# Seven block products for the product with w_in, and a cosine from 1 - 2 sin² without a clamp

## The chip, the cores and the metric

The kernel runs on one core of a Trainium2 chip. The metric is device microseconds of one execution, median of the runs shown; lower is better. The profile is taken of one further execution.

## What is computed

Three layers in a row, in fp32, over 4608 tokens of width 512:

```python
# 1. attention in chunks of 64 tokens, 64 (batch, head) pairs, head width 64
attn = softmax(q_c @ k_c.T / 8);  x = attn @ v_c          # -> [4608, 512]
# 2. RMS norm, then a gated layer, d_ff = 1536
xn = x / rms(x) * rms_g
x2 = (silu(xn @ w_gate) * (xn @ w_val)) @ w_out           # -> [4608, 512]
# 3. a cosine gate, d_ff = 2048
h = x2 @ w_in                                             # -> [4608, 2048]
out = (h * cos(h)) @ w_out2                               # -> [4608, 512]
```

The weights arrive in 64 bits and are turned into 32 on the core.

## The kernel before

The work goes in four stages, each of which writes its result to DRAM and the next reads it back: (1) attention, norm and the two gated products (lines L359 to L514); (2) the product with the first w_out (L269 under the pool `ps_c`); (3) the product with w_in and the cosine gate (L656 to L782, L798); (4) the product with the second w_out (pool `ps_c4`, L834 to L881).

Every product is made of three TensorE passes (`mm3`, L269): each fp32 operand is split into a rounded part and a remainder (`split`, L120 and L121, or L256 and L257 in `operand`: ScalarE rounds, VectorE subtracts), and high·high, high·low and low·high are added up in PSUM.

Stages 2 and 4 cut their matrices into 2 x 2 blocks and make seven block products in place of eight (the order is `PRODUCTS`); sums and differences of blocks are made on VectorE (L230 to L253) before the split, and sums of products after it (L713, L721, L841). Stage 2 takes tiles of 768 tokens, so its matmuls have 384 columns; stage 4 has 256 columns.

Stage 3 does not cut. It takes nine tiles of 512 tokens (`TILE`); for each pair of the 16 blocks of 128 rows of w_in it runs 24 matmuls of 512 columns into a PSUM tile of two banks, four such tiles in turn (`ps_h`). w_in was scaled by 1/(2 pi) beforehand (L187), so that h stands in turns. Per pair, `cosine` runs a chain over 128 x 1024 elements:

```python
nc.scalar.activation(k, h, AF.Copy, bias=0.25)                                # L798: nearest whole turn
nc.vector.scalar_tensor_tensor(r, k, -1.0, u, op0=ALU.mult, op1=ALU.add)      # L778: what is left of it
nc.vector.tensor_scalar(r, r, R_MIN, R_MAX, op0=ALU.max, op1=ALU.min)         # L779: the clamp
nc.scalar.activation(r, r, AF.Sin, scale=PI2, bias=halfpi)                    # L780: cos = sin(x + pi/2)
nc.vector.scalar_tensor_tensor(r, u, PI2, r, op0=ALU.mult, op1=ALU.mult)      # L781: h * cos(h)
```

The weights of all later stages are converted during stage 1: `w_tick` takes one raw piece at a time, eight per tile of 512 tokens, and stores the split weight in DRAM (`kept`). For w_in a piece is scaled and split (L187, L120, L121); for the two w_out the block sums are made too (L201). SBUF has 28 places for weights (`p0` to `p27`); the list `wanted` says which tile takes a place as `free` gives it back.

Stage 1 has its order on TensorE and VectorE written out by hand. In stages 2 to 4 a planner orders each engine's instructions when the program is built: it lays them out by durations of its own and gives a free engine the first one in program order that is ready by then. On the chip each engine then runs its list in that order. All DMAs go through SP's queue.

Of the kernel before, what the change touches and what calls it, by code (L numbers as in the profile page):

```python
# [9 lines left out]
F32 = mybir.dt.float32  # L10
# [10 lines left out]
P = 128  # L21
NT = 4608
# [42 lines left out]

BANK = {1: "b1", 6: "b1", 5: "b1", 3: "b1", 2: "b2", 7: "b3", 4: "b4"}
# [5 lines left out]
def kernel(  # L72
# [24 lines left out]
    gd = [dr.tile([P, N2 // 4, 4, TILE], F32, name=f"gd{t}") for t in range(NT // TILE)]  # L97
# [30 lines left out]
    wanted += [("in", f, None) for f in range(4)] + [("x2", 0, c) for c in range(2)]  # L128
    wanted += [("in", f, None) for f in range(4, N2)]
    last = [("out2", g, PLACE_B[j]) for g in range(N2 // 4) for j in PRODUCTS]  # L130
    wanted += last[:10] + [("g", g, c) for g in range(2) for c in range(2)] + last[10:]
    place_of, weight, kept, early = {}, {}, {}, {}

    def free(*tags):
        for tag in tags:
            if not wanted:
                return
            key = kind, i, k = wanted.pop(0)
            place_of[key] = tag
            if kind in ("h", "x2", "g"):  # L140
                early[key] = wp.tile([P, 2, H if kind == "h" else D], F32, tag=tag, name="a")
                rows = slice(0, 2) if kind == "h" else slice(2 * k, 2 * k + 2)
                a = {"h": hd[0][:, k], "x2": x2d[0], "g": gd[0][:, i]}[kind]
                nc.sync.dma_start(out=early[key], in_=a[:, rows, : early[key].shape[-1]])
                continue
            shape = [P, 2, D] if kind == "in" else [P, 2, 2, 2, P]
            weight[key] = wp.tile(shape, F32R, tag=tag, name="w")
            nc.sync.dma_start(out=f32(weight[key]), in_=kept[kind, i] if kind == "in" else kept[kind, i][:, k])
# [4 lines left out]
    todo_w += [("in", f, 0) for f in range(N2)]  # L153
# [4 lines left out]
    def w_load():  # L158
        if todo_w and len(raws) < 2:
# [3 lines left out]
            if kind == "in":  # L163
                nc.sync.dma_start(out=raw, in_=w2[i, 0].rearrange("p (a b) -> p a b", b=P))
# [9 lines left out]
    def w_tick():  # L174
# [9 lines left out]
        if kind == "in":  # L184
            to = pp.tile([P, 2, D], F32R, tag="pout", name="wout")
            t = t.rearrange("p a b -> p (a b)")
            nc.scalar.activation(t, t, AF.Copy, scale=INV2PI)  # L187
            split(to, t, nc.vector)
            kept[kind, i] = dr.tile([P, 2, D], F32, name=f"kin{i}")
            nc.sync.dma_start(out=kept[kind, i], in_=f32(to))  # L190
        else:
            s = pp.tile([P, 4, P], F32, tag="ps", name="wsum")

# [739 lines left out]
```

## Time and profile before

| what | value |
|---|---|
| median of 3 runs | 1741.5 us (1739.72 to 1741.79) |
| the profiled execution | 1740.49 us, span 1738.7 us |
| TensorE busy | 1702.5 us of the span (98%) |
| VectorE, ScalarE, GpSimd busy | 1176.3, 750.7, 60.7 us |
| mean granted TensorE clock | 0.995 of full speed |
| stage 3 on TensorE | from 980.3 to 1372.0 us after the span's start |

Busy time of TensorE counts overlapping matmuls once. The time outside the span, 1.8 us, is what lies before the first and after the last instruction.

### The profile page before, as it was taken

The numbers are of one execution on the slowest core, as the hardware profiler recorded it, in microseconds if no ns is written. First come the engines' busy times: TensorE is split into PE (matmuls) and PEld (weight loads), VectorE is DVE, ScalarE is ACT, GpSimd is POOL, SyncE is SP. The second block draws the span as 40 slices with busy tenths as digits, with TensorE's granted clock in tenths as the row PEclk, the third lists the DMA queues.
The fourth block names the chain that finished last, engine by engine and source line by source line (L and its number), as shares of the span: only waits on it lengthen the run. The fifth ranks groups of instructions, "written<-read, shape, count | busy, mean of one in ns | idle before, by whom it ended". The sixth has DMA issues, their size and how long they took to land.

```text
span 1738.7 us, 29349 instructions
## 1 busy us (share of the span) xinstructions
PE 1702.5 (98%) x11832; PEld 1530.8 (88%) x11832; DVE 1176.3 (68%) x1759; ACT 750.7 (43%) x1115; POOL 60.7 (3%) x104
## 2 busy tenths in 40 slices
PE   4899999999999999999999999999999999999999
PEld 4899888888888888899999988888888999999999
DVE  5775487666687741577777566666676687777775
ACT  4542444445444431344444344444454444444443
POOL 2222000000000000000000000000000000000000
PEclk8999999999999999999999999999999999999999
DMA  9423277656577738553336843333225833444430
GB/s 332 171 68 99 91 241 245 225 175 217 206 236 243 235 104 277 178 182 146 146 146 239 284 155 121 121 121 121 98 90 182 318 113 126 133 147 145 143 128 31
DMA packets 160743, 294.72 MB, mean 170 GB/s; under 512 B 10592, under 2 KB 97632, under 8 KB 156256
## 3 DMA queue, kind: packets, MB, share of 16 engines
q1 hardware_dynamic: 160608, 292.86, 49.3%
q8 instruction: 93, 1.52, 0.4%
q14 instruction: 42, 0.34, 0.1%
HBM read 173.80 MB, written 119.01 MB: 168 GB/s over the span
## 4 chain that ended last, share of the span: by engine, by line
PE 95%; issue 1%; POOL 1%; ACT 1%; DMA 1%; DVE 1%; SPq 0%; POOLq 0%
PE b L269 35%; PE h L269 23%; PE v L269 17%; PE g L269 16%; PE sc L359 1%; PE o L412 1%; PE pt L398 1%; PE tr L450 1%; POOL w L121 1%; DMA qk<-in_qk_dram 1%; DMA w<-kin 0%; POOL rs L430 0%; ACT p L381 0%; ACT L381 0%; ACT xo L256 0%
## 5 line engine op out<-in xcount | busy, mean ns | idle before, releaser
L269 PE MATMUL h<-xt,w 128*128 128x512 f32 x1728 | 391.9, 389 | 0.0
L269 PEld LDWEIGHTS h<-xt,w 128*128 128x128 f32 x1728 | 324.3, 188 | 67.3
L269 PEld LDWEIGHTS b<-w,xo 128*128 128x128 f32 x3024 | 363.0, 192 | 0.1
L269 PE MATMUL b<-w,xo 128*128 128x256 f32 x3024 | 363.0, 283 | 0.0
L269 PE MATMUL v<-xt,w 128*128 128x512 f32 (+1 forms) x1488 | 324.4, 367 | 3.6 <-DVE xn L437 1.8
L269 PE MATMUL g<-xt,w 128*128 128x512 f32 (+1 forms) x1488 | 320.8, 365 | 0.8 <-ACT xt L452 0.7
L269 PEld LDWEIGHTS g<-xt,w 128*128 128x128 f32 x1488 | 257.6, 191 | 44.8 <-ACT xt L452 1.1
L269 PEld LDWEIGHTS v<-xt,w 128*128 128x128 f32 x1488 | 253.7, 191 | 46.1 <-DVE xn L437 2.0
L269 PE MATMUL b<-xo,w 128*128 128x384 f32 x1512 | 263.2, 334 | 3.6 <-ACT xo L256 3.5
L269 PEld LDWEIGHTS b<-xo,w 128*128 128x128 f32 x1512 | 262.1, 188 | 4.7 <-ACT xo L256 4.5
L257 DVE TENSOR_TENSOR xo<-rawg,xo 128x512 fp32r<-128x512 f32 x204 | 135.5, 688 | 66.6 <-ACT xo L256 66.5
L256 ACT CAST xo<-rawg 128x512 fp32r<-128x512 f32 x204 | 121.8, 620 | 126.0 <-PE b L269 82.1
L501 DVE TENSOR_TENSOR h<-sg,v 128x512 f32<-128x512 f32 (+1 forms) x124 | 76.2, 615 | 138.6 <-PE v L269 123.2
L500 ACT ACTIVATE sg<-g 128x512 f32<-128x512 f32 (+1 forms) x124 | 66.9, 541 | 237.1 <-PE g L269 223.5
L780 ACT ACTIVATE r<-r,halfpi 128x1024 f32<-128x1024 f32 x72 | 83.0, 1153 | 134.4 <-DVE r L779 134.2
L781 DVE SCALAR_TENSOR_TENSOR r<-h,r 128x1024 f32<-128x1024 f32 x72 | 88.1, 1224 | 74.2 <-ACT r L780 73.7
L778 DVE SCALAR_TENSOR_TENSOR r<-k,h 128x1024 f32<-128x1024 int32 x72 | 87.9, 1220 | 69.3 <-ACT k L798 69.1
L256 ACT CAST xo<-rawh 128x768 fp32r<-128x768 f32 x102 | 81.3, 834 | 97.4 <-DMA rawh<-hd 53.5
L257 DVE TENSOR_TENSOR xo<-rawh,xo 128x768 fp32r<-128x768 f32 x102 | 92.9, 953 | 40.4 <-ACT xo L256 40.3
L798 ACT ACTIVATE k<-h 128x1024 int32<-128x1024 f32 x72 | 73.9, 1026 | 79.5 <-PE h L269 79.5
L256 ACT CAST xo<-tmp 128x512 fp32r<-128x512 f32 (+1 forms) x54 | 37.4, 692 | 61.6 <-DVE tmp L230 36.9
L779 DVE TENSOR_SCALAR r<-r 128x1024 f32<-128x1024 f32 x72 | 49.9, 693 | 2.1
(86 smaller groups left out, 1230.4 us busy)
## 6 DMA issues: line engine op xcount, KB each, us to landing
gd<-r SPq DMA_DIRECT2D x72, 512.0 KB, 2.6
rawg<-gd SPq DMA_DIRECT2D x34, 1024.0 KB, 7.1
kout<-wout SPq DMA_DIRECT2D x56, 448.0 KB, 4.5
w<-kout SPq DMA_DIRECT2D x49, 512.0 KB, 4.9
hd<-h SPq DMA_DIRECT2D x46, 512.0 KB, 4.7
rawh<-hd SPq DMA_DIRECT2D x15, 1536.0 KB, 9.1
qk<-in_qk_dram SPq DMA_DIRECT2D x36, 512.0 KB, 6.1
wraw<-in_w_dram SPq DMA_DIRECT2D x112, 128.0 KB, 2.7
```

Source lines behind the costliest of these rows:

```text
L121: eng.tensor_tensor(to[:, 1], a, f32(to[:, 0]), op=ALU.subtract)
L256: nc.scalar.copy(hi, a)
L257: nc.vector.tensor_tensor(lo, a, f32(hi), op=ALU.subtract)
L269: nc.tensor.matmul(acc, a, b, start=first and k == 0 and q == 0, stop=k == n - 1 and q == 2, skip_group_check=True)
L359: nc.tensor.matmul(sc[part(h ^ b), 2 * hp + (c ^ b), :], t[part(h), 0, hp, part(c)], t[part(h), 1, hp, part(c)], start=True, stop=True,)
L500: nc.scalar.activation(sg, acc[0], AF.Silu)
L501: nc.vector.tensor_tensor(h, sg, acc[1], op=ALU.mult)
L778: nc.vector.scalar_tensor_tensor(r, k, -1.0, u, op0=ALU.mult, op1=ALU.add)
L779: nc.vector.tensor_scalar(r, r, R_MIN, R_MAX, op0=ALU.max, op1=ALU.min)
L780: nc.scalar.activation(r, r, AF.Sin, scale=PI2, bias=halfpi)
L781: nc.vector.scalar_tensor_tensor(r, u, PI2, r, op0=ALU.mult, op1=ALU.mult)
L798: nc.scalar.activation(k, h, AF.Copy, bias=0.25)
```

## The change

Stage 3 is cut like the others. It takes six tiles of 768 tokens, and w_in in four groups of 512 columns of h; for each of the 24 pairs of tile and group (a *group* below) it makes seven block products of 12 matmuls, 384 columns each. The order is 1, then the products 4 and 3 of the group before, then 2, 6, 5, 7. Product sums run up in PSUM bank pair `b1` (1, 1+6, 1+6+7, 1+6+7+4; two buffers), `b2` (2) and `b5` (5, then 5+3; one buffer each). ScalarE copies `b1` out on the way (`z1`, `z16`, `z167`); VectorE adds these to `b2` and `b5` and so gives three of the group's four result blocks, in SBUF; the fourth is `b1` itself. The operands of the next tile's products are made one by one behind the products of the last group of a tile.

For three of the four blocks the cosine is made another way: k is the nearest whole number, q = u - k, then Sin at half the angle, Square, and one VectorE instruction for (2 pi)(2 sin² - 1) u; there is no clamp and no bias. w_in is scaled by -1/(2 pi), so u is minus the turn. The fourth block keeps the old chain. All of these work on 128 x 768 elements.

Preparing w_in now makes the block sums as for the w_out; its weights in SBUF are 28 pieces of 512 KB in place of 16. `gd` is kept in pieces of 1536 tokens in place of 512. The first five operands of stage 4 (`op4`) get places among the weights.

The diff, cut to its core:

```diff
+THIRD = (1, 2, 6, 5, 7, 4, 3)
+BANK3 = {1: "b1", 6: "b1", 7: "b1", 4: "b1", 2: "b2", 5: "b5", 3: "b5"}
...
     x2d = [dr.tile([P, ND, PIECE], F32, name=f"x2d{q}") for q in range(NPIECE)]
-    gd = [dr.tile([P, N2 // 4, 4, TILE], F32, name=f"gd{t}") for t in range(NT // TILE)]
+    gd = [dr.tile([P, N2 // 4, 4, PIECE], F32, name=f"gd{q}") for q in range(NPIECE)]
...
     wanted[3:3] = [("h", 0, g) for g in range(N1 // 4)]
-    wanted += [("in", f, None) for f in range(4)] + [("x2", 0, c) for c in range(2)]
-    wanted += [("in", f, None) for f in range(4, N2)]
+    third_w = [("in", g, PLACE_A[j]) for g in range(N2 // 4) for j in THIRD]
+    wanted += third_w[:7] + [("x2", r, c) for r in range(2) for c in range(2)] + third_w[7:]
     last = [("out2", g, PLACE_B[j]) for g in range(N2 // 4) for j in PRODUCTS]
-    wanted += last[:10] + [("g", g, c) for g in range(2) for c in range(2)] + last[10:]
+    wanted += last[:10] + [("g", g, c) for g in range(2) for c in range(2)]
+    wanted += [("op4", n, None) for n in range(AHEAD)] + last[10:]
...
     todo_w = [("out1", i, half) for i in range(N1 // 2) for half in range(2)]
-    todo_w += [("in", f, 0) for f in range(N2)]
+    todo_w += [("in", i, half) for i in range(N2 // 2) for half in range(2)]
...
             raw = wp.tile([P, 4, P], U64, tag=f"p{24 + flip[0]}", name="wraw")
             if kind == "in":
-                nc.sync.dma_start(out=raw, in_=w2[i, 0].rearrange("p (a b) -> p a b", b=P))
+                m, e = 4 * (i // 2) + half, i % 2
+                for n, (f, c) in enumerate(((m, e), (m, e + 2), (m + 2, e + 2), (m + 2, e))):
+                    nc.sync.dma_start(out=raw[:, n, :], in_=w2[f, 0][:, c * P : (c + 1) * P])
...
         t = f32(t)
         if kind == "in":
-            to = pp.tile([P, 2, D], F32R, tag="pout", name="wout")
-            t = t.rearrange("p a b -> p (a b)")
-            nc.scalar.activation(t, t, AF.Copy, scale=INV2PI)
-            split(to, t, nc.vector)
-            kept[kind, i] = dr.tile([P, 2, D], F32, name=f"kin{i}")
-            nc.sync.dma_start(out=kept[kind, i], in_=f32(to))
+            nc.scalar.activation(t, t, AF.Copy, scale=-INV2PI)
+        s = pp.tile([P, 4, P], F32, tag="ps", name="wsum")
...
+            ops = ((t[:, 3, :], t[:, 0, :], ALU.subtract), (t[:, 2, :], s[:, 0, :], ALU.subtract))
+            ops += ((t[:, 2, :], t[:, 3, :], ALU.subtract), (t[:, 1, :], s[:, 1, :], ALU.subtract))
         else:
...
-                nc.sync.dma_start(out=kept[kind, g][:, :, e, h, half], in_=f32(to[:, h]))
+            ops = ((t[:, 3, :], t[:, 2, :], ALU.add), (s[:, 0, :], t[:, 0, :], ALU.subtract))
+            ops += ((t[:, 0, :], t[:, 3, :], ALU.subtract), (t[:, 1, :], s[:, 1, :], ALU.subtract))
+        for n, (a, b, op) in enumerate(ops):
...
+        to = pp.tile([P, 2, 7, P], F32R, tag="pout", name="wout")
+        split(to[:, :, 0:3, :], t[:, :3, :], nc.vector)
+        split(to[:, :, 3:7, :], s, nc.vector)
...
+    def fetch3(s):
+        if s == 0:
+            raw3[s] = {(r, c): early["x2", r, c] for r in range(2) for c in range(2)}
+        elif s < NB:
+            t = third_p.tile([P, 4, T], F32, tag="raw", name="rawx2", bufs=1)
+            raw3[s] = blocks(t, False)
+            c = s * T % PIECE
+            nc.sync.dma_start(out=t, in_=x2d[s * T // PIECE][:, :, c : c + T])
...
+    def operand3(s, j):
+        b = raw3[s]
+        if j == 6:
+            raw3[s, "t"] = t = third_p.tile([P, 2, H], F32, tag="tmp", name="tmp", bufs=1)
+            nc.vector.tensor_tensor(t, b[0, 1], b[0, 0], op=ALU.subtract)
+            nc.vector.tensor_tensor(b[0, 0], b[1, 1], t, op=ALU.subtract)
+        elif j == 7:
+            nc.vector.tensor_tensor(b[0, 1], b[1, 1], b[0, 1], op=ALU.subtract)
+        elif j == 4:
+            nc.vector.tensor_tensor(b[1, 0], b[1, 0], b[0, 0], op=ALU.subtract)
+        a = raw3[s, "t"] if j == 5 else b[{1: (0, 0), 2: (1, 0), 6: (0, 0), 7: (0, 1), 4: (1, 0), 3: (1, 1)}[j]]
+        pool = third_p if j in (1, 2, 6) else left_p
+        o = pool.tile([P, 2, 2, H], F32R, tag="x3", name="x3", bufs=4)
+        split(o, a, nc.vector)
+        ops3[s, j] = o
+        if j == 3:
+            if s == 0:
+                free(*(place_of["x2", r, c] for r in range(2) for c in range(2)))
+            else:
+                fetch3(s + 1)
+    def ahead3(n):
+        while made3[0] < min(len(seq3), n):
+            operand3(*seq3[made3[0]])
+            made3[0] += 1
...
                     second.close()
-                    xt_p = third.enter_context(tc.tile_pool(name="xt3", bufs=2, side="right", reuse_waits="tile"))
+                    third_p = third.enter_context(tc.tile_pool(name="right3", bufs=1, side="right", reuse_waits="tile"))
                     fetch3(0)
-                    split3(0, 0)
-                    split3(0, 2)
+                    fetch3(1)
+                    ahead3(3)
...
-            nc.sync.dma_start(out=t, in_=gd[s][:, g])
+            c = s * TILE % PIECE
+            nc.sync.dma_start(out=t, in_=gd[s * TILE // PIECE][:, g, :, c : c + TILE])
...
     def operand4(s, j, g):
-        tmp = xo_p.tile([P, 2, H4], F32, tag="tmp", name="tmp", bufs=1) if j == 7 else None
-        ops4[s, j, g] = operand(j, raw4[s, g], tmp, lambda: parts(xo_p, H4), True)
+        n = made4[0]
+        if n < AHEAD:
+            tmp = left_p.tile([P, 2, H], F32, tag="r", name="tmp", bufs=4)[:, :, :H4] if j == 7 else None
+            o = wp.tile([P, 2, 2, H4], F32R, tag=place_of["op4", n, None], name="xo")
+            to = o[:, 0], o[:, 1]
+        else:
+            tmp = xo_p.tile([P, 2, H4], F32, tag="tmp", name="tmp", bufs=1) if j == 7 else None
+            to = parts(xo_p, H4)
+        ops4[s, j, g] = operand(j, raw4[s, g], tmp, lambda: to, True)
...
         st.enter_context(third)
-        tp = st.enter_context(tc.tile_pool(name="tp3", bufs=2, side="right", reuse_waits="tile"))
-        ps_h = st.enter_context(tc.tile_pool(name="ps_h", bufs=4, space=PSUM, reuse_waits="tile"))
...
-        def cosine(keep):
-            while len(late) > keep:
-                u, k, i, f = late.pop(0)
-                r = tp.tile([P, 2, D], F32, tag="r", name="r", bufs=4)
-                nc.vector.scalar_tensor_tensor(r, k, -1.0, u, op0=ALU.mult, op1=ALU.add)
-                nc.vector.tensor_scalar(r, r, R_MIN, R_MAX, op0=ALU.max, op1=ALU.min)
-                nc.scalar.activation(r, r, AF.Sin, scale=PI2, bias=halfpi)
-                nc.vector.scalar_tensor_tensor(r, u, PI2, r, op0=ALU.mult, op1=ALU.mult)
-                nc.sync.dma_start(out=gd[i][:, f // 4, f % 4 : f % 4 + 2, :], in_=r)
...
-        for i in range(ntile):
...
-            for f in range(0, N2, 2):
-                h = ps_h.tile([P, 2, D], F32, tag="h", name="h2")
-                for e in range(2):
-                    w = weight["in", f + e, None]
-                    c = [slice(d * P, (d + 1) * P) for d in range(ND)]
-                    x = xts[i]
-                    mm3(h[:, e], [(w[:, 0, c[d]], w[:, 1, c[d]], x[:, 0, d], x[:, 1, d]) for d in range(ND)], True)
-                k = tp.tile([P, 2, D], I32, tag="k", name="k")
-                nc.scalar.activation(k, h, AF.Copy, bias=0.25)
-                late.append((h, k, i, f))
-                cosine(0)
-                if i == ntile - 1:
-                    free(place_of["in", f, None], place_of["in", f + 1, None])
-                    if f == 0:
+        left_p = st.enter_context(tc.tile_pool(name="left3", bufs=1, reuse_waits="tile"))
+        ps_h = st.enter_context(tc.tile_pool(name="ps_h", bufs=1, space=PSUM, reuse_waits="tile"))
+        ahead3(7)
...
+        def multiply(acc, s, j, g, first):
+            w = weight["in", g, PLACE_A[j]]
+            x = ops3[s, j]
+            for p in range(2):
+                mm3(
+                    acc[:, p],
+                    [(w[:, e, 0, p], w[:, e, 1, p], x[:, 0, e], x[:, 1, e]) for e in range(2)],
+                    first,
+                )
+            if s == NB - 1:
+                free(place_of["in", g, PLACE_A[j]])
+            if g == G3 - 1 and j != 1:
+                ahead3(made3[0] + 1)
...
+        def opened(bank, bufs=1):
+            return ps_h.tile([P, 2, D], F32, tag=bank, name=bank, bufs=bufs)[:, :, :H]
+        def saved(acc, tag):
+            t = left_p.tile([P, 2, H], F32, tag=tag, name=tag)
+            nc.scalar.copy(t, acc)
+            return t
+        def total(acc, part):
+            t = left_p.tile([P, 2, H], F32, tag="u", name="u", bufs=3)
+            nc.vector.tensor_tensor(t, acc, part, op=ALU.add)
+            return t
...
+        def turn(u, s, g, r, c, whole):
+            q = left_p.tile([P, 2, H], F32, tag="r", name="r", bufs=4)
+            k = q.bitcast(I32)
+            if whole:
+                nc.scalar.copy(k, u)
+                nc.vector.scalar_tensor_tensor(q, k, -1.0, u, op0=ALU.mult, op1=ALU.add)
+                nc.scalar.activation(q, q, AF.Sin, scale=math.pi)
+                nc.scalar.activation(q, q, AF.Square, scale=math.sqrt(2 * PI2))
+                nc.vector.scalar_tensor_tensor(q, q, -PI2, u, op0=ALU.add, op1=ALU.mult)
+            else:
+                nc.scalar.activation(k, u, AF.Copy, bias=0.25)
+                nc.vector.scalar_tensor_tensor(q, k, -1.0, u, op0=ALU.mult, op1=ALU.add)
+                nc.vector.tensor_scalar(q, q, R_MIN, R_MAX, op0=ALU.max, op1=ALU.min)
+                nc.scalar.activation(q, q, AF.Sin, scale=PI2, bias=halfpi)
+                nc.vector.scalar_tensor_tensor(q, u, -PI2, q, op0=ALU.mult, op1=ALU.mult)
+            t0 = s * T + c * H
+            o = t0 % PIECE
+            nc.sync.dma_start(out=gd[t0 // PIECE][:, g, 2 * r : 2 * r + 2, o : o + H], in_=q)
...
+        def tail(s, g, z, z16):
+            multiply(z["b1"], s, 4, g, False)
+            turn(z["b1"], s, g, 1, 0, False)
+            multiply(z["b5"], s, 3, g, False)
+            turn(total(z["b5"], z16), s, g, 0, 1, True)
...
+        rest = None
+        for s in range(NB):
+            for g in range(G3):
+                z = {"b1": opened("b1", 2)}
+                multiply(z["b1"], s, 1, g, True)
+                z1 = saved(z["b1"], "z1")
+                if rest:
+                    tail(*rest)
+                z["b2"] = opened("b2")
+                multiply(z["b2"], s, 2, g, True)
+                turn(total(z["b2"], z1), s, g, 0, 0, True)
+                multiply(z["b1"], s, 6, g, False)
+                z16 = saved(z["b1"], "z16")
+                z["b5"] = opened("b5")
+                multiply(z["b5"], s, 5, g, True)
+                multiply(z["b1"], s, 7, g, False)
+                turn(total(z["b5"], saved(z["b1"], "z167")), s, g, 1, 1, True)
+                rest = s, g, z, z16
+                if g == G3 - 2:
+                    ahead3(made3[0] + 1)
+                if s == NB - 1:
+                    if g == G3 - 2:
                         fetch4(0, 0)
                         fetch4(0, 1)
-                    elif f >= 6:
-                        ahead4((f - 4) // 2)
-                if f in (8, 10):
-                    split3(i + 1, f - 8 if f == 8 else 2)
-                if f == 10:
-                    fetch3(i + 2)
-            if i == 0:
-                free(place_of["x2", 0, 0], place_of["x2", 0, 1])
+                        ahead4(2)
+                    elif g == G3 - 1:
+                        ahead4(4)
+        tail(*rest)
+        ahead4(AHEAD)
...
-        st.enter_context(fourth)
...
+        xo_p = st.enter_context(tc.tile_pool(name="xo4", bufs=8, reuse_waits="tile"))
...
+            if n < AHEAD:
+                free(place_of["op4", n, None])
```

## Rows read from the trace of the kernel before

**Rows 1.** The page's first part: busy us, share of the span, instructions, by engine.

```profile
PE 1702.5 (98%) x11832; PEld 1530.8 (88%) x11832; DVE 1176.3 (68%) x1759; ACT 750.7 (43%) x1115; POOL 60.7 (3%) x104
```

**Rows 2.** The chain that ended last, its piece for stage 3: start, us, what.

```profile
980.31 391.72 PE h L269 x1728
```

**Rows 3.** Windows, stages 2 to 4: us, then busy of PE, PEld, DVE, ACT, POOL.

```profile
713.50:980.00 266.50, 262.86 (x1513) 261.89 (x1512) 198.57 (x220) 118.12 (x149) 0.00 (x0) 1.00 0.50 177
980.00:1372.00 392.00, 392.00 (x1732) 324.60 (x1731) 248.39 (x244) 174.66 (x167) 0.00 (x0) 1.00 0.40 145
1372.00:1738.70 366.70, 362.90 (x3025) 362.70 (x3023) 272.68 (x424) 163.67 (x279) 0.00 (x0) 1.00 0.38 132
```

**Rows 4.** Groups by line and form, matmuls and weight loads: busy us, mean ns | idle.

```profile
L269 PE MATMUL h<-xt,w 128*128 128x512 f32 x1728 | 391.9, 389 | 0.0
...
L269 PE MATMUL b<-xo,w 128*128 128x384 f32 x1512 | 263.2, 334 | 3.6 <-ACT xo L256 3.5
L269 PEld LDWEIGHTS b<-xo,w 128*128 128x128 f32 x1512 | 262.1, 188 | 4.7 <-ACT xo L256 4.5
```

**Rows 5.** Groups by line and form: the cosine chain of stage 3, 1024 elements.

```profile
L781 DVE SCALAR_TENSOR_TENSOR r<-h,r 128x1024 f32<-128x1024 f32 x72 | 88.1, 1224 | 74.2 <-ACT r L780 73.7
L778 DVE SCALAR_TENSOR_TENSOR r<-k,h 128x1024 f32<-128x1024 int32 x72 | 87.9, 1220 | 69.3 <-ACT k L798 69.1
L780 ACT ACTIVATE r<-r,halfpi 128x1024 f32<-128x1024 f32 x72 | 83.0, 1153 | 134.4 <-DVE r L779 134.2
...
L798 ACT ACTIVATE k<-h 128x1024 int32<-128x1024 f32 x72 | 73.9, 1026 | 79.5 <-PE h L269 79.5
...
L779 DVE TENSOR_SCALAR r<-r 128x1024 f32<-128x1024 f32 x72 | 49.9, 693 | 2.1
```

**Rows 6.** Groups by line and form: copies and sums of 768, casts of 512 and 1024.

```profile
L256 ACT CAST xo<-rawh 128x768 fp32r<-128x768 f32 x102 | 81.3, 834 | 97.4 <-DMA rawh<-hd 53.5 <-PE b L269 19.7 <-DVE rawh L253 12.5
...
L121 DVE TENSOR_TENSOR xt<-rawx,xt 128x1024 fp32r<-128x1024 f32 x16 | 19.4, 1219 | 1.6 <-ACT xt L120 1.6
...
L721 DVE TENSOR_TENSOR x<-b,s 128x768 f32<-128x768 f32 x18 | 17.2, 955 | 9.9 <-ACT s L711 5.2 <-DMA x2d<-x 4.6
...
L120 ACT CAST xt<-rawx 128x1024 fp32r<-128x1024 f32 x16 | 15.9, 1047 | 2.4 <-DMA rawx<-x2d 2.4
...
L711 ACT COPY s<-b 128x768 f32<-128x768 f32 x18 | 14.4, 802 | 15.0 <-PE b L269 15.0
```

**Rows 7.** Timeline of stage 3, a split inside a cosine chain: start, us, engine.

```profile
1067.49 1.03 ACT L798 ACTIVATE k<-h 128x1024 int32<-128x1024 f32 x1 [1.24 <-PE h L269]
...
1068.55 1.22 DVE L778 SCALAR_TENSOR_TENSOR r<-k,h 128x1024 f32<-128x1024 int32 x1 [1.05 <-ACT k L798]
1069.69 1.22 DVE L121 TENSOR_TENSOR xt<-rawx,xt 128x1024 fp32r<-128x1024 f32 x1
1070.82 0.69 DVE L779 TENSOR_SCALAR r<-r 128x1024 f32<-128x1024 f32 x1
```

**Rows 8.** Timeline of ScalarE in stage 1: Silu, Square, Silu, then a table load.

```profile
304.44 0.60 ACT L500 ACTIVATE sg<-g 128x512 f32<-128x512 f32 x1 [4.21 <-PE g L269]
...
306.92 0.58 ACT L426 ACTIVATE xn<-o 128x512 f32<-128x512 f32 x1
...
311.20 0.60 ACT L500 ACTIVATE sg<-g 128x512 f32<-128x512 f32 x1 [3.03 <-PE g L269]
...
318.65 1.28 ACT L381 ACT_TABLE_LOAD   x1
```

**Rows 9.** Windows, stage 1: w_in prepared in the first, second w_out in the second.

```profile
331.00:396.00 65.00, 65.00 (x538) 53.59 (x537) 40.93 (x71) 30.84 (x54) 2.97 (x8) 1.00 0.54 188
...
527.00:593.00 66.00, 66.00 (x537) 54.58 (x527) 54.04 (x114) 30.58 (x54) 2.97 (x8) 1.00 0.77 243
```

**Rows 10.** DMA issues: queue, count, KB each, median us from issue to landing.

```profile
rawg<-gd SPq DMA_DIRECT2D x34, 1024.0 KB, 7.1
...
rawx<-x2d SPq DMA_DIRECT2D x8, 1024.0 KB, 6.0
```

More of the change, by code (lines that the diff above doesn't have):

```diff
@@ L139, in free @@
             place_of[key] = tag
+            if kind == "op4":
+                continue
             if kind in ("h", "x2", "g"):
[L141 to L144, printed above, removed]
+                early[key] = wp.tile([P, 2, D if kind == "g" else H], F32, tag=tag, name="a")
+                if kind == "h":
+                    a = hd[0][:, k, 0:2, :H]
+                elif kind == "x2":
+                    a = x2d[0][:, 2 * i : 2 * i + 2, k * H : (k + 1) * H]
+                else:
+                    a = gd[0][:, i, 2 * k : 2 * k + 2, :D]
+                nc.sync.dma_start(out=early[key], in_=a)
                 continue
-            shape = [P, 2, D] if kind == "in" else [P, 2, 2, 2, P]
-            weight[key] = wp.tile(shape, F32R, tag=tag, name="w")
-            nc.sync.dma_start(out=f32(weight[key]), in_=kept[kind, i] if kind == "in" else kept[kind, i][:, k])
+            weight[key] = wp.tile([P, 2, 2, 2, P], F32R, tag=tag, name="w")
+            nc.sync.dma_start(out=f32(weight[key]), in_=kept[kind, i][:, k])
     todo_w = [("out1", i, half) for i in range(N1 // 2) for half in range(2)]
-    todo_w += [("in", f, 0) for f in range(N2)]
+    todo_w += [("in", i, half) for i in range(N2 // 2) for half in range(2)]
     todo_w += [("out2", i, half) for i in range(N2 // 2) for half in range(2)]
@@ new lines, in w_tick @@
+        for n, (a, b, op) in enumerate(ops):
+            nc.vector.tensor_tensor(s[:, n, :], a, b, op=op)
+        to = pp.tile([P, 2, 7, P], F32R, tag="pout", name="wout")
+        split(to[:, :, 0:3, :], t[:, :3, :], nc.vector)
+        split(to[:, :, 3:7, :], s, nc.vector)
+        g, e = i // 2, i % 2
+        if (kind, g) not in kept:
+            kept[kind, g] = dr.tile([P, 7, 2, 2, 2, P], F32, name=f"k{kind}{g}")
+        for h in range(2):
+            nc.sync.dma_start(out=kept[kind, g][:, :, e, h, half], in_=f32(to[:, h]))
@@ L645 @@
     third = ExitStack()
[L646 to L662 removed]
+    raw3, ops3 = {}, {}
+    seq3 = [(s, j) for s in range(NB) for j in THIRD]
+    made3 = [0]
+    def fetch3(s):
[30 more added lines that the diff above has]
+            made3[0] += 1
     with ExitStack() as st:
@@ new lines @@
+        ps_h = st.enter_context(tc.tile_pool(name="ps_h", bufs=1, space=PSUM, reuse_waits="tile"))
+        ahead3(7)
+        G3 = N2 // 4
+        def multiply(acc, s, j, g, first):
[11 more added lines that the diff above has]
+                ahead3(made3[0] + 1)
```

42 lines of the change are left out of this document (2 added, 40 removed).

## The prediction

> **What bounds the kernel now.** First the page's busy times: TensorE is busy for 1702.5 us of the 1738.7 us span, VectorE for 1176.3, ScalarE for 750.7 [rows 1]. Then the chain of work that ended last: it runs through stage 3 as one unbroken piece of TensorE, 391.72 us of 1728 matmuls [rows 2]. The windows by stage say the same: in stage 3 TensorE is busy for 392.0 of 392.0 us, VectorE for 248.4 (63%), ScalarE for 174.7 (45%) [rows 3]. So a microsecond taken from stage 3's matmuls is a microsecond off the kernel as long as the other two engines keep up, and the question is whether they do once they carry more.
>
> **TensorE's work.** Stage 3 now runs 1728 matmuls of 512 columns in 391.9 us, 226.8 ns each [rows 4]. Afterwards there are 24 groups x 7 products x 12 = 2016 matmuls of 384 columns. Stage 2 runs that form: 1512 in 263.2 us, 174.1 ns each [rows 4], also back to back. 2016 x 174.1 = 350.9 us, which is **41.0 us less**. One product lasts 12 x 0.174 = 2.09 us and a group 14.62 us.
>
> The mean weight load is 188 ns, longer than that distance; but 1512 of them took only 262.1 us together [rows 4], so they overlap and 174.1 stands. The Trainium skill (Perfetto Trace Analysis, section Identifying the Most-Contended Engine) says to judge TensorE's headroom by the busy share of its weight loads and not of its matmuls; by it stage 3 at 324.6 of 392 us has room, and a stage of 384 columns has none (261.9 of 266.5 [rows 3]). Were the loads serial at 188 ns, the stage would take 379 us and the saving would be 13 us; the trace speaks against it.
>
> **ScalarE and VectorE, per group.** Prices for 768 elements: a copy from PSUM 0.80 (L711) and from SBUF 0.834 (L256), a sum on VectorE 0.955 (L721) [rows 6]. The casts of 1024 and 768 elements differ by 0.21 us [rows 6], so L798 at 1.026 becomes 0.81 and Sin with its bias at 1.153 becomes 0.94 [rows 5]. Sin without a bias column, and Square, do not occur on SBUF data; they lie between a plain copy, 0.83, and 0.94; I take 0.84, as the operand column is gone. The two-input forms L778 and L781 cost on 1024 elements what a plain sum does, 1.22 against 1.219 [rows 5, 6], so 0.955 on 768. The clamp at 0.693 [rows 5] is between 0.52 (in proportion) and 0.69; I take 0.56.
>
> ScalarE: three copies of bank sums 2.41, three new cosines of copy, Sin and Square 7.54, one old cosine 1.75, a quarter of a tile's seven operand roundings 1.46; together 13.2 us of the group's 14.62 (90%).
>
> VectorE: three sums 2.87, two instructions for each new cosine 5.73, the old cosine 1.91 + 0.56, a quarter of a tile's eleven operand instructions (seven remainders, four block differences) 2.63; together 13.7 us (94%). Over the stage that is 329 us, more than the 248.4 of now, and still below 350.9. So neither engine bounds the stage by its sum; but the cover is thin.
>
> **What can be late.** PSUM gives short deadlines, counted in products. The copy z16 must end before product 7 goes on in `b1`: only product 5 lies between, 2.09 us for a copy of 0.80. z167 must end before product 4: product 1 lies between, 2.09 again. Before product 3 VectorE must have added `b5` to z167: 4.18 us for 0.80 + 0.955. Before product 5 it must have added the old `b5` to the old z16: 4.18 us. Behind a late copy stand first TensorE's product, and on ScalarE's list all that was put after it.
>
> The planner fills gaps: in stage 3 now it set a split between L778 and L779 of one chain [rows 7], so the four cosines of a group will interleave and not run one after the other. But it takes what comes first in program order, and there the cosines of products 4, 3 and 2 come before z16. I lay out three successive groups by hand, each engine taking the first ready instruction at the prices above, 0.05 us from engine to engine (L778 starts 1.06 us after L798 starts its 1.03 [rows 7]). In the first, z16 runs from 10.9 to 11.7 us after the group began, in time for 12.53. In the second, the Sin and Square of block 2 stand before z167, which ends 2.2 us into the next group: product 4 waits 0.2. In the third, Sin and Square of block 3 and the copy for block 2 stand before z16, which runs from 13.2 to 14.0: product 7 waits 1.3. The fourth begins as the first did. That is 1.5 us in three groups, 0.5 each, **12 us** in 24. Bounds: nothing (all copies in time), and two waits of 1.3 in every group, 62 us.
>
> Operands do not spread evenly. Of a tile's eleven VectorE instructions seven fall behind products 2, 6, 5 and 7 of its last group: 11.07 + 7 x 0.955 = 17.8 us against 14.62, 3.1 us too much. The following group has 14.0, the two after 11.1 and 12.0, so the backlog is worked off there, but what is late in between is a sum with a deadline. Five tiles have a successor: between 0 and 5 x 3.1 = 16 us. I take **10**, nearer the upper end, because the final cosine instructions, which could wait, are first in program order.
>
> **Stage 3's edges.** The last group's old cosine holds two banks that stage 4's third and fourth products want: from product 4's end its chain is 0.81 + 0.955 + 0.56 + 0.94 + 0.955 = 4.2 us and queueing, against product 3 (2.09) and two products of stage 4 (362.9 us / 3024 x 12 = 1.44 each [rows 3]), 5.0 in all. I take **1 us**, from 0 to 3. The start loses nothing that I see: three operands are made in stage 2, where VectorE is busy for 198.6 of 266.5 us [rows 3].
>
> **At nothing.** Preparing w_in now costs VectorE what the second w_out does already (four block sums and a second remainder more). While that was prepared, eight pieces in some 66 us, VectorE was busy for 54.0 of 66 us and TensorE for all 66; with w_in, 40.9 of 65 [rows 9], so a piece grows by some 1.6 us. The four small loads in place of one and the two stores in place of one go through SP's queue as in that window. If the cover were gone, 16 x 1.6 = 26 us would show. Reading `gd` back in rows of 2 KB has the form of `rawx`, 6.0 us to landing against 7.1 of `rawg` now [rows 10]. Stage 4's own wait for data does not grow by this.
>
> **Table loads, a rule against the change.** Sin and Square alternate on ScalarE. In stage 1 Silu, Square and Silu run without a load between them, and the next load, 1.28 us, stands at Exp's line [rows 8]; in stage 3 Sin, which comes after Silu, has none at its line. So Silu, Square and Sin share a set and nothing is added.
> The Trainium skill (ScalarE: Activation LUTs, section Table sets: the hidden batching unit) says to batch activations by table set, since a function from another set brings a load; this trace agrees, at 1.28 us for each change to Exp.
>
> **Sum.** 1740.5 of the profiled execution - 41.0 + 12 + 10 + 1 = 1722.5. The median of the runs stands 1.0 above that execution: **1723.5 us**. A run of this kernel tells apart about 0.2%, 3.5 us.
>
> **Rivals.**
> Full gain: every copy meets its deadline. For it speaks that both sums are under 14.62; against it the deadlines of 2.09 us at loads of 90 and 94%. 1741.5 - 41 + 0 to 3 = 1701 to 1704.
> No change: waits eat all of the gain, 1.5 to 1.85 us per group, operands included (break-even is 391.9 / 24 - 14.62 = 1.71). 1738 to 1745.
> Slower: ScalarE's strict order. If the planner's durations differ from the chip's, z16 and z167 stand behind two or three cosine instructions in every group and each is 1.3 us late: 24 x 2.6 = 62. 1741.5 - 41 + 62 + 1 = 1764. It decides from 1.71 us of waiting per group. For it speaks that before, four PSUM tiles in turn kept TensorE clear of a chain of 5.3 us (the sum of rows 5), and now a single copy stands in its way. Were the chains of a group run strictly in turn, 4.2 + 3 x 5.4 = 20.4 us, the stage would take 490 us and the kernel 1840; rows 7 speak against that.
> Table loads after all, for each Sin and each Square of the 72 new cosines: 144 x 1.28 = 184 us on ScalarE, 316 + 184 = 500 for the stage, 1850 in all; rows 8 exclude it but for 1 in 100.
> It does not do what it says: weight loads serial at 188 ns, 379 us, 1728.5 before any wait; 2 in 100.
>
> **Chances.** Forecast (1705 to 1738) 0.53, full gain 0.20, weight loads 0.02, no change 0.09, slower 0.15, table loads 0.01. So faster 0.75, within 0.2% 0.09, slower 0.16. The range from 1700 (full gain) to 1744 (the end of no change) leaves out the slower cases, 0.16; the forecast's own range is 1705 to 1738.
>
> **What will show it.** Matmuls of 384 columns at 174 ns where they run back to back, 2016 of them; VectorE at about 329 us and ScalarE at 316 us in the stage; no table load there. TensorE's idle time should stand at products waiting for ScalarE's copies z16 and z167 and for VectorE's sums of `b5`, some 0.5 us a group and more at every fourth. I am wrong if that idle time is under 5 or over 40 us, if a cosine instruction costs over 1 us, or if stage 1 or stage 4 grows.

## The result and the profile after

The changed kernel takes 1703.37 us (median of 4 runs, 1700.25 to 1703.65) against 1740.61; the ratio is 0.9782, 95% interval 0.9765 to 0.9799. That is 37.2 us less, where 18 were forecast: the waits that should have eaten half of the gain are not there.

The page's first part:

```profile
PE 1664.8 (98%) x12120; PEld 1557.0 (91%) x12120; DVE 1256.9 (74%) x1959; ACT 876.6 (52%) x1347; POOL 60.5 (4%) x104
```

The waits of TensorE from 978 to 1345 us, in which stage 3 lies (engine, line, what it waited for: us in total, times, longest):

```profile
PE b L275 <- ACT z L825: 0.9, 1, 0.9
```

One wait of 0.9 us, in the very last group, for a bank copy (L825 is the copy, L275 the matmul): less than the 5 us under which the prediction had called itself wrong. The windows of stage 3 and stage 4 (us, then busy of PE, PEld, DVE, ACT, POOL, that is of TensorE, its weight loads, VectorE, ScalarE and GpSimd, each with its count of instructions; then the granted clock, the share of the DMA engines and GB/s):

```profile
981.50:1333.60 352.10, 351.16 (x2014) 348.23 (x2013) 297.01 (x349) 289.47 (x375) 0.00 (x0) 1.00 0.47 164
1333.60:1701.70 368.10, 364.23 (x3030) 363.70 (x3028) 277.15 (x433) 166.57 (x286) 0.00 (x0) 1.00 0.43 145
```

The groups by line and form (busy us, mean ns of one):

```profile
L275 PE MATMUL b<-x,w 128*128 128x384 f32 x2016 | 352.0, 335 | 0.9 <-ACT z L825 0.9
...
L842 DVE SCALAR_TENSOR_TENSOR r<-r,u 128x768 f32<-128x768 f32 x72 | 68.6, 953 | 22.4 <-ACT r L841 22.1
...
L841 ACT ACTIVATE r<-r 128x768 f32<-128x768 f32 x72 | 61.0, 847 | 1.1
L840 ACT ACTIVATE r<-r 128x768 f32<-128x768 f32 x72 | 60.8, 844 | 31.6 <-DVE r L839 31.5
...
L825 ACT COPY z<-b 128x768 f32<-128x768 f32 x72 | 56.6, 794 | 8.9 <-PE b L275 7.1
...
L847 ACT ACTIVATE r<-r,halfpi 128x768 f32<-128x768 f32 x24 | 22.5, 937 | 1.3 <-DVE r L846 1.3
...
L846 DVE TENSOR_SCALAR r<-r 128x768 f32<-128x768 f32 x24 | 13.3, 555 | 0.2
```

Stage 3 shrank from 391.7 us [rows 2] to 352.8 (TensorE's first matmul of stage 3 at 981.56, of stage 4 at 1334.32), 39 us. It begins 1.3 us later than before, and stage 4 takes 0.7 us longer; that makes the 37.0 us between the spans. The prices hold to 0.02 us: Sin 0.844 (L840), Square 0.847 (L841), a bank copy 0.794, the clamp 0.555, Sin with a bias 0.937, a two-input instruction 0.953. What does not hold is the load: in the window VectorE is busy for 297 us and ScalarE for 289, not 329 and 316.

### The profile page after: what moved, and what is told of

Read it like the earlier page. It is cut to its first block, busy times and chain, and to the rows that moved or that the text cites. A ratio compares the mean times of both kernels' runs of the same rounds, so it can differ in the third digit from the quotient of the medians.

```text
span 1701.7 us, 30479 instructions
## 1 busy us (share of the span) xinstructions
PE 1664.8 (98%) x12120; PEld 1557.0 (91%) x12120; DVE 1256.9 (74%) x1959; ACT 876.6 (52%) x1347; POOL 60.5 (4%) x104
## 4 chain that ended last, share of the span: by engine, by line
PE 94%; DMA 2%; ACT 1%; DVE 1%; issue 1%; POOL 1%; SPq 0%; POOLq 0%; ACTq 0%; DVEq 0%
PE b L275 56%; PE v L275 17%; PE g L275 17%; PE o L418 1%; PE sc L365 1%; DMA raw<-in_w_dram 1%; PE tr L456 1%; PE pt L404 1%; DMA qk<-in_qk_dram 1%; POOL w L124 1%; DMA v<-in_v_dram 0%; DMA hd<-h 0%; ACT xo L262 0%; POOL rs L436 0%; ACT L387 0%
## 5 line engine op out<-in xcount | busy, mean ns | idle before, releaser
L275 PE MATMUL b<-w,xo 128*128 128x256 f32 x3024 | 363.5, 283 | 0.1
L275 PEld LDWEIGHTS b<-w,xo 128*128 128x128 f32 x3024 | 363.2, 192 | 0.4 <-DVE xo L263 0.3
L275 PE MATMUL b<-x,w 128*128 128x384 f32 x2016 | 352.0, 335 | 0.9 <-ACT z L825 0.9
L275 PEld LDWEIGHTS b<-x,w 128*128 128x128 f32 x2016 | 348.9, 188 | 3.9 <-ACT z L825 3.1
L275 PE MATMUL v<-xt,w 128*128 128x512 f32 (+1 forms) x1488 | 324.6, 367 | 3.6 <-DVE xn L443 1.7
L275 PE MATMUL g<-xt,w 128*128 128x512 f32 (+1 forms) x1488 | 322.3, 366 | 0.8 <-ACT xt L458 0.7
L275 PEld LDWEIGHTS g<-xt,w 128*128 128x128 f32 x1488 | 259.0, 192 | 44.9 <-ACT xt L458 1.1
L275 PEld LDWEIGHTS v<-xt,w 128*128 128x128 f32 x1488 | 253.8, 191 | 46.2 <-DVE xn L443 2.0
L275 PE MATMUL b<-xo,w 128*128 128x384 f32 x1512 | 263.2, 334 | 2.6 <-ACT xo L262 2.5
L275 PEld LDWEIGHTS b<-xo,w 128*128 128x128 f32 x1512 | 262.1, 188 | 3.7 <-ACT xo L262 3.5
L842 DVE SCALAR_TENSOR_TENSOR r<-r,u 128x768 f32<-128x768 f32 x72 | 68.6, 953 | 22.4 <-ACT r L841 22.1
L839 DVE SCALAR_TENSOR_TENSOR r<-r,u 128x768 f32<-128x768 int32 x72 | 68.6, 953 | 12.5 <-ACT r L838 12.4
L840 ACT ACTIVATE r<-r 128x768 f32<-128x768 f32 x72 | 60.8, 844 | 31.6 <-DVE r L839 31.5
L830 DVE TENSOR_TENSOR u<-b,z 128x768 f32<-128x768 f32 x72 | 68.5, 952 | 7.6 <-ACT z L825 7.4
L838 ACT CAST r<-u 128x768 int32<-128x768 f32 x72 | 59.8, 830 | 9.7 <-DVE u L830 9.3
```

Of the source, the lines that this page charges most:

```text
L275: nc.tensor.matmul(acc, a, b, start=first and k == 0 and q == 0, stop=k == n - 1 and q == 2, skip_group_check=True)
L830: nc.vector.tensor_tensor(t, acc, part, op=ALU.add)
L838: nc.scalar.copy(k, u)
L839: nc.vector.scalar_tensor_tensor(q, k, -1.0, u, op0=ALU.mult, op1=ALU.add)
L840: nc.scalar.activation(q, q, AF.Sin, scale=math.pi)
L842: nc.vector.scalar_tensor_tensor(q, q, -PI2, u, op0=ALU.add, op1=ALU.mult)
```

## The experiments

All are edits of the changed kernel in stage 3, but for the first, which is one of the kernel before. Times are medians; "over" is the time over the changed kernel's 1703.4 us. The ratios are known to some 0.0015, 2.6 us, and the changed kernel's own as well, so a single difference in the last column is known to some 4 us.

| run | us | ratio to before (95%) | over |
|---|---|---|---|
| cosine_alone | 1740.5 | 1.0002 (0.9992 to 1.0011) | |
| old_cosine | 1714.4 | 0.9842 (0.9824 to 0.9860) | 11.0 |
| more_work | 1704.0 | 0.9785 (0.9771 to 0.9800) | 0.6 |
| vector_work | 1703.4 | 0.9781 (0.9765 to 0.9798) | 0.0 |
| z16_exposed | 1703.3 | 0.9782 (0.9765 to 0.9798) | -0.1 |
| scalar_in_order | 1917.5 | 1.1016 (1.0994 to 1.1038) | 214 |
| all_in_order | 2010.7 | 1.1552 (1.1529 to 1.1575) | 307 |
| tensor_in_order | 1710.1 | 0.9817 (0.9802 to 0.9831) | 6.8 |
| z16_tensor_in_order | 1740.7 | 0.9996 (0.9987 to 1.0005) | 37.3 |
| more_work_tied | 1708.8 | 0.9813 (0.9796 to 0.9829) | 5.4 |
| vector_work_tied | 1731.0 | 0.9939 (0.9924 to 0.9954) | 27.6 |
| premises | 1717.3 | 0.9859 (0.9842 to 0.9876) | 13.9 |
| copies_behind | 1733.9 | 0.9962 (0.9948 to 0.9975) | 30.6 |
| premises_copies_behind | 1792.8 | 1.0298 (1.0254 to 1.0342) | 89.4 |

**The halves of the change.** cosine_alone:

```diff
-                nc.vector.tensor_scalar(r, r, R_MIN, R_MAX, op0=ALU.max, op1=ALU.min)
-                nc.scalar.activation(r, r, AF.Sin, scale=PI2, bias=halfpi)
-                nc.vector.scalar_tensor_tensor(r, u, PI2, r, op0=ALU.mult, op1=ALU.mult)
+                if whole:  # three of four pairs
+                    nc.scalar.activation(r, r, AF.Sin, scale=math.pi)
+                    nc.scalar.activation(r, r, AF.Square, scale=math.sqrt(2 * PI2))
+                    nc.vector.scalar_tensor_tensor(r, r, -PI2, u, op0=ALU.add, op1=ALU.mult)
```

> The kernel before with only the second half of the change: three of four pairs of blocks get the cosine from 1 - 2 sin^2, in the old tiles of 512 tokens. TensorE's work is that of before. Theory A (an engine's load counts, its instructions overlap): VectorE and ScalarE have room, 1741 us within 4. Rival (the chains of successive pairs run in turn): the new chain is 1.03 + 1.22 + 1.15 + 1.15 + 1.22 = 5.8 us against 5.44 us of matmuls per pair, 72 pairs, so some 20 to 26 us more for the 54 to 72 pairs, 1760 to 1767 us.

No difference: the copy of the next pair starts while VectorE still ends the last one, so the longer chain costs nothing. By itself the new cosine is worth nothing. old_cosine makes the seven products alone:

```diff
-            if whole:
+            if False:
```

> The changed kernel with the old cosine (copy with bias, clamp, Sin with bias) for all four blocks: seven products alone. Per group VectorE gets three clamps more (three times about 0.5 us) and ScalarE three Squares less (three times about 0.75): VectorE from 12.4 to 13.9 of 14.7 us, ScalarE from 12.1 to 9.8. Theory A (the waits I forecast are absent because the real loads are 84 and 82%): at 95% of VectorE waits appear, 1708 to 1722 us. Theory B (the planner's order keeps the bank copies ahead, whatever the load below 100%): 1703 to 1707 us.

It is 11 us slower than the whole change. Its profiled execution was the fastest of four, 1709.6 us, so it shows some 6 of these. Its window from 981.5 to 1333 us (the changed kernel has 296.69 for VectorE there):

```profile
981.50:1333.00 351.50, 343.67 (x1966) 340.03 (x1965) 323.96 (x410) 238.50 (x299) 0.00 (x0) 1.00 0.45 157
```

The longest of TensorE's waits in the stage:

```profile
PE b L275 <- DVE r L848: 4.7, 5, 0.9
PE b L275 <- ACT z L825: 4.0, 5, 1.1
```

VectorE is at 324 of 351.5 us, and waits do appear, at the tiles' ends. So the new cosine earns 6 to 11 us once the products are there: it takes three clamps a group off VectorE.

**Load, first try.** more_work puts this pair of useless instructions in four places of each group; vector_work has two on VectorE in each place:

```diff
+                nc.vector.tensor_tensor(gamma[:, :256], gamma[:, :256], gamma[:, :256], op=ALU.subtract)
+                nc.scalar.copy(gamma[:, 256:], gamma[:, 256:])
```

> The changed kernel with four useless instructions of 256 elements more on VectorE and four on ScalarE in each group, on a tile that nothing reads any more: by 0.33 and 0.30 us each the loads come to 13.7 and 13.3 us per group, those that the prediction was made with. Theory A (load): waits as predicted, 12 to 22 us, 1713 to 1726 us. Theory B (order): under 5 us, 1703 to 1708 us.

> The changed kernel with eight useless VectorE instructions of 256 elements in each group. If an instruction loads its engine for its distance to the next one (0.33 us each, 0.87 for one of 768), VectorE has 15.0 us per group and bounds the stage: 24 x (15.0 - 14.7) = 8 us and some waiting, 1709 to 1726 us. If it loads it for its whole duration (0.416 and 0.953), VectorE has 17.0 us per group: 24 x 2.3 = 56 us, 1759 us.

Nothing changed, but the runs tell nothing about load. The instructions of the tile in more_work (duration ns min/median/max, first and last start us):

```profile
L866 ACT COPY gamma<-gamma x24: 401/407/427, 643.9 to 689.3; 128x256 f32<-128x256 f32 x24
L865 DVE TENSOR_TENSOR gamma<-gamma x24: 418/425/427, 643.9 to 693.0; 128x256 f32<-128x256 f32 x24
```

They waited for nothing, and so the planner had them run at 644 to 694 us, at the end of stage 1.

**Load, tied.** The same, reading a tile that the group has just made; vector_work_tied has two on VectorE and none on ScalarE:

```diff
... (the same two lines behind the copy z1)
             nc.vector.tensor_tensor(t, acc, part, op=ALU.add)
+            nc.vector.tensor_tensor(gamma[:, :256], t[:, 0, :256], t[:, 1, :256], op=ALU.subtract)
+            nc.scalar.copy(gamma[:, 256:], t[:, 1, :256])
```

> The changed kernel with four useless instructions of 256 elements on VectorE and four on ScalarE in each group, each reading a tile that this group has just made (a bank copy or a sum), so that they can't run before stage 3 as those of the first try did. VectorE comes to some 13.7 and ScalarE to 13.3 us per group of 14.7, the loads of the prediction. Theory A (load): waits as predicted, 12 to 22 us, 1713 to 1726 us. Theory B (order): under 5 us, 1703 to 1708 us.

> The changed kernel with eight useless VectorE instructions of 256 elements in each group, each reading a tile that this group has just made. If an instruction loads its engine for the distance to the next one (0.33 us each, 0.87 for one of 768 elements), VectorE has 15.0 us per group: 8 us over, and some waiting, 1711 to 1730 us. If it loads it for its whole duration (0.42 and 0.953), VectorE has 17.0 us per group and the kernel is at 1759 us.

The window from 1000 to 1294 us of the changed kernel:

```profile
1000.00:1294.00 294.00, 293.96 (x1688) 291.88 (x1687) 252.22 (x296) 245.47 (x318) 0.00 (x0) 1.00 0.41 142
```

The same window of more_work_tied:

```profile
1000.00:1294.00 294.00, 289.53 (x1652) 285.42 (x1651) 277.01 (x368) 260.61 (x390) 0.00 (x0) 1.00 0.39 135
```

The same window of vector_work_tied:

```profile
1000.00:1294.00 294.00, 280.96 (x1575) 279.11 (x1574) 283.12 (x424) 230.15 (x296) 0.00 (x0) 0.97 0.35 124
```

With 84 matmuls to a group, VectorE has 252.22 x 84 / 1688 = 12.6 us per group in the changed kernel, 14.1 with the tied work (ScalarE 12.2 and 13.3), and 15.1 in the last, more than the 14.6 that TensorE needs there at its full clock. So more_work_tied carries at least the loads of the prediction, and loses 5.4 us, not 22; TensorE's waits in its profile come to 5.4 us as well. In vector_work_tied, where they stand in pairs, eight instructions added 2.5 us, 0.32 each, though each lasts 0.42 (four single ones in more_work_tied 0.39 each). It ends 1 us above the range of the first reading and 28 us under the second: an instruction loads its engine for its distance to the next. Part of its 27.6 us is TensorE's clock, 0.97 in the window.

**The deadlines and TensorE's list.** z16_exposed:

```diff
-THIRD = (1, 2, 6, 5, 7, 4, 3)
+THIRD = (1, 2, 6, 7, 5, 4, 3)
...
-                z["b5"] = opened("b5")
-                multiply(z["b5"], s, 5, g, True)
                 multiply(z["b1"], s, 7, g, False)
+                z167 = saved(z["b1"], "z167")
+                z["b5"] = opened("b5")
+                multiply(z["b5"], s, 5, g, True)
... (the last sum takes z167)
```

> The changed kernel with the products in the order 2, 6, 7, 5 in place of 2, 6, 5, 7: no product lies between the copy z16 and product 7. If the deadlines in the banks are real, TensorE waits in every group for the copy, 0.80 us and what it waits for on ScalarE (0.1 to 0.9 us): 22 to 40 us, 1725 to 1743 us. If they do not bind: 1703 us within 4.

Nothing was lost. The list of TensorE in the built program shows why (products 6, 5, 7, 5 of one group; the bank pair written, the operand read, the number of matmuls):

```
MATMUL b_10260<-x_9936,w 128x384 x12
MATMUL b_10365<-x_10028,w 128x384 x6
MATMUL b_10260<-x_10025,w 128x384 x12
MATMUL b_10365<-x_10028,w 128x384 x6
```

The planner cut product 5 in two and filled the wait for the copy with one half. In the changed kernel it does the like in the first three groups (in the first with a whole product), once in the last tile and where a tile ends, there with 2 to 4 matmuls of a following product; in the other groups TensorE's list is the written order. Strict order on TensorE takes that away:

```diff
         rest = None
+        st.enter_context(tc.manual_schedule(engines={ET.PE}))
         for s in range(NB):
```

> The changed kernel with TensorE's list in strict program order during stage 3 (1, 4, 3, 2, 6, 5, 7), the other two engines planned as before. In the changed kernel the planner had moved some of TensorE's matmuls too: in some groups 2 to 10 matmuls of the next product stand ahead of one whose bank is still being copied. Theory C (the deadlines that I counted in products do not bind because TensorE's list was planned around them): waits as predicted come back, 10 to 22 us, 1713 to 1726 us. Theory B (ScalarE's and VectorE's lists are enough): under 5 us, 1703 to 1708 us.

> The run with the order 2, 6, 7, 5 again, with TensorE's list in strict program order. There the planner had put half of product 5 between products 6 and 7, and nothing was lost. If the deadline of z16 is real, now TensorE stands for the copy in every group: 0.80 us and 0.1 to 0.9 for its start, 22 to 40 us, 1725 to 1743 us. If not: 1703 us within 4.

With the products as in the change it costs 6.8 us, less than theory C wanted. TensorE's waits:

```profile
PE b L275 <- ACT z L825: 7.4, 7, 3.9
```

3.9 us are one wait in the first group, where product 6 needs the copy z1; the others are 0.5 to 0.9 us at a tile's end. With z16 exposed it costs 37.3 us; TensorE's waits there:

```profile
PE b L275 <- ACT z L825: 31.4, 25, 2.8
```

25 waits, one in each group and a second in the first, 1.26 us each on the mean. The deadline is real; the planner's list of TensorE evades it.

**ScalarE's and VectorE's lists.** The same line, TensorE in order, with `ET.Activation` added, then with `ET.DVE` too:

> The changed kernel with ScalarE's list in strict program order during stage 3, so that z16 stands behind Sin and Square of block 2; the loads are the same. Theory B (order): z16 ends some 5.2 us after product 2 (sum 0.95, copy 0.83, difference 0.95, Sin 0.85, Square 0.85, copy 0.80) against a deadline of 4.18, so at least 1.1 us of waiting per group, 26 us, and more where the chains push each other: 1730 to 1790 us. Theory A alone (load): 1703 to 1708 us.

> The changed kernel with VectorE's list in strict program order as well: the four chains of a group follow one another. By the prediction's sum 4.2 + 3 x 5.4 = 20.4 us per group, 490 us for the stage against 353: 1840 us, 1800 to 1860. If the planner's interleaving is worth little: under 1730 us.

Both are far slower than expected. In scalar_in_order a group takes 14.7 + 214 / 24 = 23.6 us on the mean. I had reckoned only z16. The trace of one group (start, us, what; from the copy z16 to the next group's):

```profile
1202.27 0.78 ACT L825 COPY z<-b 128x768 f32<-128x768 f32 x1
1203.10 16.25 PE L275 MATMUL b<-x,w 128*128 128x384 f32 x84 [5.14 <-ACT z L825]
1206.91 0.80 ACT L825 COPY z<-b 128x768 f32<-128x768 f32 x1 [3.86 <-PE b L275]
...
1223.73 0.78 ACT L825 COPY z<-b 128x768 f32<-128x768 f32 x1
```

It takes 21.5 us. Behind z16 ScalarE stands for 3.9 us until product 7, which had to wait for that copy, has run (2.09 us at the full clock; the last section shows why it took longer); only then can it copy z167 (1206.91) and go through the four chains and z1 one after another, until the next z16 at 1223.73. Groups at a tile's end are longer, as the operands' roundings stand in between. all_in_order has 27.5 us per group; what it adds I have not taken apart. Both show that the gain stands on the planner's interleaving, since TensorE's order alone costs 6.8 us.

**Putting the premises back.** premises is more_work_tied with TensorE in order:

> The tied extra work and TensorE's strict program order together: the loads (13.7 and 13.3 us per group) and the order that the prediction reckoned with. If those two premises are all that was wrong, the waits of the prediction appear, 22 us: 1721 to 1731 us. If the hand layout itself made the waits too long, the two effects only add up, 5.4 + 6.8 us: 1713 to 1718 us.

It comes to 13.9 us: within the noise the two effects add up (5.4 + 6.8), and the forecast's 22 do not appear. One assumption was left: in the hand layout the bank copies stand behind Sin and Square of the earlier chains. ScalarE's timeline in the changed kernel (start, us, line):

```profile
1120.13 0.85 ACT L840 ACTIVATE r<-r 128x768 f32<-128x768 f32 x1 [0.33 <-DVE r L839]
1120.89 0.79 ACT L825 COPY z<-b 128x768 f32<-128x768 f32 x1
1121.57 0.85 ACT L841 ACTIVATE r<-r 128x768 f32<-128x768 f32 x1
1122.31 0.82 ACT L838 CAST r<-u 128x768 int32<-128x768 f32 x1
1124.47 0.85 ACT L840 ACTIVATE r<-r 128x768 f32<-128x768 f32 x1 [1.33 <-DVE r L839]
1125.22 0.79 ACT L825 COPY z<-b 128x768 f32<-128x768 f32 x1
1125.90 0.85 ACT L841 ACTIVATE r<-r 128x768 f32<-128x768 f32 x1
```

The first copy here (L825) is z16, the second z167. Each stands between a Sin (L840) and its Square (L841), which comes before the copy in program order. In the lists of the built program z16 stands ahead of block 3's Square in 16 of 23 groups (in 9 between Sin and Square, in 7 ahead of the Sin as well), and z167 ahead of block 2's Square in 16 of 24. copies_behind forbids just that, in every group, and the planner lays out the rest anew; premises_copies_behind adds it to premises (`sq` lists the Squares so far; the last but one is that of block 3, the last that of block 2):

```diff
-            nc.scalar.copy(t, acc)
+            back = {"z16": 2, "z167": 1}.get(tag, 0)
+            with tc.issue_after(sq[-back].ins) if back and len(sq) >= back else ExitStack():
+                nc.scalar.copy(t, acc)
```

> The changed kernel with two bank copies held back on ScalarE's list, as in the prediction's layout: z16 never before the Square of block 3, z167 never before the Square of block 2. In the changed kernel the planner sets a copy between Sin and Square of a chain in most groups, because the copy is ready there earlier. The rest is planned as before. If that place of the copies is the third reason for the missing waits: 5 to 15 us, 1708 to 1718 us. If TensorE's list, planned around them, makes up for it: 1703 us within 4.

> The run with both premises (tied extra work, TensorE in program order), and the two copies held back as well: all three of the prediction's assumptions. If they explain the forecast, the 22 us of waits are there, 1722 to 1732 us. If the hand layout was too long for another reason, it stays at 1717 within 4.

Alone it costs 30.6 us, twice what I had expected at most and nearly all of the change's gain; with the two premises 89.4. TensorE's waits in copies_behind:

```profile
PE b L275 <- DVE u L834: 11.8, 13, 1.4
PE b L275 <- ACT z L829: 6.1, 5, 3.0
PE b L275 <- DVE r L852: 3.3, 5, 0.7
```

Most of them are not for the copy but for VectorE's sums (L834), which come behind the late copies: the lateness goes through the group. In premises_copies_behind they are for the copies:

```profile
PE b L275 <- ACT z L829: 67.8, 25, 3.5
```

## Why the prediction was wrong

Its direction and its bound were right: TensorE stayed the bound, the matmul term of 41.0 us came in at 39 for the whole stage, no table was loaded in stage 3, the weight loads of 188 ns overlapped (348.9 us for all 2016), the prices held, stage 1 hid the dearer preparation of w_in (TensorE busy for 553.5 of 553.5 us from 160 to 713.5), and `rawg` lands in 6.3 us, near the 6.0 of its model [rows 10]. The rival called full gain, which had 0.20, is what happened. The step that failed is "What can be late", the terms of 12 and 10 us. They measured 0.9 together, for three reasons; each is shown by a run that takes it away, but what each was worth of the 22 us is not.

**The place of the copies.** "It takes what comes first in program order, and there the cosines of products 4, 3 and 2 come before z16." But the planner takes it only among what is ready by its own times, and on its lists a waiting copy slips in behind the Sin, or ahead of it. On the chip a Square starts 0.88 us after its Sin,

```profile
1107.09 0.85 ACT L840 ACTIVATE r<-r 128x768 f32<-128x768 f32 x1 [0.84 <-DVE r L839]
1107.97 0.85 ACT L841 ACTIVATE r<-r 128x768 f32<-128x768 f32 x1
```

and a copy that does not depend on the Sin 0.76 after it (1120.13, 1120.89). That the planner's own times have such a difference, and so see the copy ready first, is presumed. To put the copies behind the Squares costs 30.6 us, the largest of the three.

**TensorE's list.** I counted deadlines in products and let TensorE stand when one was missed, though the text said that the planner orders every engine. It had shifted matmuls into the waits: 6.8 us. Five of the waits that come back, 0.5 to 0.7 us each and 2.6 in all, stand at a tile's end, where the term of 10 us had looked for them.

**The loads.** I added up durations. Instructions that follow each other without a dependency overlap, and the trace of before has it: VectorE in stage 2, six splits in a row, each 0.953 us long,

```profile
733.03 5.30 DVE L257 TENSOR_TENSOR xo<-rawh,xo 128x768 fp32r<-128x768 f32 x6
```

take 5.30 us, (5.30 - 0.953) / 5 = 0.87 apart. So a group had 12.6 and 12.2 us of work and not 13.7 and 13.2. For the matmuls I had taken busy time over count, and for the two other engines the mean of one. With the load back, 5.4 us of waits come.
The Trainium skill (Perfetto Trace Analysis, section Optimizing Scalar/DVE Operations) says that the second half of an instruction's data-access overhead, the write acknowledgement, overlaps with the next one, so that its profiled latency is longer than its engine-busy time. The trace agrees: 0.953 against 0.87 on VectorE; on ScalarE a Square of 0.85 at 1121.57 is followed at 1122.31, 0.74 later.

The size of 22 us is not rescued by its premises: with all three in force the chip loses 89.4 us, most of it in waits for the copies (67.8 us) and some 14 us by a lower clock (last section). The layout followed three groups and found them 0, 0.2 and 1.3 us late; what it says of the next sums shows no lateness taken on into them. The held-back copies may be stricter than the layout was, as they stand behind the Squares in every group. As far as the three edits stand for the three premises, the forecast came from two errors against each other: premises that made too many waits, and a layout that made them too short. What made the layout too short no run shows, so that part is argued.

## What to carry to other kernels

Take an engine's load as busy time over count from a stretch where it runs without a gap, never as count times mean duration, and do it for every engine alike. Where a planner orders the lists, a deadline counted in program order does not give the wait, which was 0.9 us where the planner was free and 89.4 us over where three of its liberties were taken: look which instruction it lets slip in, and test by pinning one engine's list, or one instruction's place. Useless work that is to load a stage must read something that the stage makes.

## What the runs showed of the hardware

In scalar_in_order TensorE stood again and again for some 5 us (5.14 us before 1203.10, 5.21 before 1224.56), and the granted clock was at the lower level when it went on. Two windows behind the first of these waits (the first figure behind the engines is the clock):

```profile
1203.10:1206.30 3.20, 3.20 (x10) 3.20 (x11) 0.26 (x1) 0.00 (x0) 0.00 (x0) 0.52 0.34 123
1207.00:1219.00 12.00, 12.00 (x71) 12.00 (x70) 7.85 (x9) 6.81 (x9) 0.00 (x0) 1.00 0.14 49
```

In the first, at 0.52, a matmul of 384 columns loads TensorE for some 0.32 us (3.20 / 10), in the second, at 1.00, some 0.17 (12.00 / 71). The levels are 1.2 and 2.4 GHz. Over a longer stretch the figure is a mean of both:

```profile
1200.00:1300.00 100.00, 70.16 (x347) 68.88 (x348) 53.84 (x61) 52.18 (x66) 0.00 (x0) 0.86 0.24 87
```

In copies_behind, whose waits are 1.4 us or less but for a few, it stayed at 1.00 from 1000 to 1294 us. vector_work_tied, with waits up to 3.4 us, has 0.97 in the window shown, and premises_copies_behind, with waits up to 3.5 us, 0.96 in the same window. What that costs shows in its groups of 84 matmuls:

```profile
1159.97 16.41 PE L275 MATMUL b<-x,w 128*128 128x384 f32 x84 [2.43 <-ACT z L829]
1178.50 14.84 PE L275 MATMUL b<-x,w 128*128 128x384 f32 x84 [2.12 <-ACT z L829]
```

Nine groups took 16.4 us like the first of these, 1.6 us each or 14 us in all. So a long wait can be paid twice, which none of my expectations had counted.
